# Strided v in four transfers of 32 partitions, and the weights' own parts stored in two transfers

## The chip, the cores and the metric

The kernel runs on one core of one Trainium2 chip. The core has a matrix engine (PE in the profile; its weight loads are PEld), three engines for elementwise work (DVE, ACT, POOL) and SyncE (SP), which here does nothing but issue transfers. Transfers between device memory and the core's working memory run on 16 DMA engines. The working memory has 128 partitions; a tile is named by its partitions times its bytes in each.

The metric is the device time of one execution in microseconds (us), as the median of several runs. Less is better.

## What is computed

Attention over 8 batches, 8 heads, 576 positions and a head size of 64, with two kinds of mask, and behind it a feed-forward layer with three input matrices whose products are joined by a maximum. In the reference (cut):

```python
mask_local = (rel >= 0) & (rel < stride)                     # heads 0 to 3, stride 32
mask_strided = (rel >= 0) & (pos[None, :] % stride == pos[:, None] % stride)   # heads 4 to 7
scores = np.where(masks[None, :, :, :], scores, -1000000000.0)
scores = scores - np.max(scores, axis=-1, keepdims=True)
attn = np.exp(scores)
attn = attn / (np.sum(attn, axis=-1, keepdims=True) + 1e-09)
attn_out = np.matmul(attn, v).astype(np.float32)

x = attn_out.transpose(0, 2, 1, 3).reshape(B * S, H * D)     # 4608 x 512
h = np.maximum(np.maximum(x @ w1, x @ w2), x @ w3)           # 512 x 768 each
return (h @ w_out).astype(np.float32)                        # 768 x 512
```

## The kernel before

**Units.** The attention is done in 32 units, each a batch `b` and a pair of heads `p`. Pairs 2 and 3 have the strided mask, pairs 0 and 1 the local one; in each batch the order is 2, 3, 0, 1, so units 4, 5, 8, 9, 12, 13 and so on are strided. For a unit, `load_qk` (L238) and `load_v` (L256) issue the transfers, `scores` (L303) makes the products of q and k on PE, DVE and ACT turn them into probabilities, and `values` (L428) multiplies by v. `paired_queries` (L292) rearranges q on ACT for strided units. `leading` and `rest` (L498 to L505) copy the result, on ACT and DVE, into the feed-forward's input. Each unit has a tile for q and k and one for v; of each there are two (plus two for units 2 and 3), so the loads of unit n + 2 are issued when unit n has been used.

**Numbers in parts.** Every float32 number that PE works on is the sum of two shorter ones, a high and a low part, and a product of two such numbers is three matmuls. The weights arrive as 64-bit words from which ACT, DVE and POOL build the two parts (`convert_begin` at L157 to `convert_end` at L199). There are 24 weight tiles, w0 to w17 for the three input matrices and six more for the output matrix. ACT reads a tile first at L164 as soon as it has landed, and works in order.

**Three stretches.** First, LOADS (L54) is a list of transfers, written out by hand, that SP issues at the start: q and k, v, and weights, step by step. Each token such as `v4` asks `load_v` for its next transfer; `q`, `w` and `v` mean qk, weights and v. OPENING (L58) is a list of computing steps in a fixed order, in which the weights are converted, the first units are done and the first 512 tokens pass through the feed-forward (`ff_in` at L518, `ff_max`, `ff_out`, `ff_store`). Second, a loop (L729) takes the next 512 tokens through it, with one unit of the attention between the products now and then (`burst`, L650). Third, `supers` (L772) takes the other 3,584 tokens in four groups with a scheme that needs seven products instead of eight for a 2 x 2 block of matrices. Before it, and between its groups, `conversion` (L679) prepares the group's input on ACT (L686) and DVE (L689, L692).

**Weights for the third stretch.** The scheme needs sums and differences of the weights. `build_sums` (L571), `build_mix`, `build_high` and `build_low` make them in nine builds in the first two stretches and store them in device memory, in `scratch`, a tensor of 9 builds x 128 partitions x 7 products x 512 numbers. Of the seven products four (S4, S2, S1, S3) are stored by `build_high` and `build_low` at L611 and L613. Three are the weights' own parts: A12 and A11, the two halves of one weight tile, are stored at L575, and A22, a half of another, at L576. `load_next` (L666) streams one product, 256 KB, back into a tile `w_stream` at L674; eight are kept ahead, and each of the third stretch's products (six matmuls at L778) uses one and calls `load_next` again. Outputs leave by transfers that ACT issues, at L563 and L876.

**Order.** `pin` keeps the program's order on each engine. SP is thus one queue: an issue that has to wait holds all that stand behind it. ACT's issues stand between its copies in the same way.

**The two places of the change.** A strided unit's v is, in device memory, a tensor of 32 rows (and unused ones up to 128) x 2 heads x 32 groups x 64 numbers. In working memory partition 32j + r holds, of row r, the groups 8j to 8j + 7 of both heads: 2 x 2 KB. For batch 0, where only 18 rows are read, `load_v` issues four transfers of 18 partitions (L285); from batch 1 on it issues one of 128 partitions (L279), whose source has j outermost. The own parts at L575 go out as they lie: 4 KB a partition, the high part of both halves and then the low part of both; `load_next` then picks the halves of A12 and A11 out of that order (L671), in two pieces of 1 KB a partition, while other products are read as one piece of 2 KB (L673).

Of the kernel before, what the change touches and what calls it, by code (L numbers as in the profile page):

```python
# [7 lines left out]
F32 = mybir.dt.float32  # L8
# [17 lines left out]
NI = S // STRIDE  # L26
# [7 lines left out]
PAIRED = 1  # L34
# [15 lines left out]
A12, A11, A22, S4, S2, S1, S3 = range(7)  # L50
# [21 lines left out]
def fused_kernel(ctx, tc, qT, kT, qk_loc, qk_str, v_loc, v_str, m_loc, m_str, w1, w2, w3, w_out, out):  # L72
    nc = tc.nc
# [9 lines left out]
    scratch = dram.tile([9, P, 7, 512], F32, name="scratch")  # L83
# [16 lines left out]
    pin = tc.keep_in_program_order  # L100
# [17 lines left out]
    for sign in (1, -1):  # L118
        pin(nc.gpsimd.affine_select(
            out=unit, in_=unit, pattern=[[-sign, P]], base=0, channel_multiplier=sign, compare_op=ALU.is_ge, fill=0.0  # L120
# [23 lines left out]
    def load_weights(count):  # L144
        for _ in range(count):
            i, j = sources.pop(0)
            raw = (wo if i is None else wt).tile([P, 1024], I32, name=f"w{i}_{j}")
            if i is None:
                pin(nc.sync.dma_start(out=raw, in_=w_out.bitcast(I32)[j * P : (j + 1) * P, :]))
            else:  # L150
                src = (w1, w2, w3)[i].bitcast(I32)[:, j * 2 * P : (j + 1) * 2 * P]
                pin(nc.sync.dma_start(
                    out=raw.rearrange("p (c f) -> p c f", c=NKC), in_=src.rearrange("(c p) f -> p c f", p=P)
                ))
            raws.append((raw, i, j))
# [19 lines left out]
    converted, kept = [], {}  # L175
# [80 lines left out]
    def load_v(n):  # L256
        if n >= len(units):
            return
        b, p = units[n]
        if n in (2, 3):  # L260
            vt = io_early.tile([P, 2 * (MB + 1) * D], F32, name="v_t", bufs=2)
        else:
            vt = io.tile([P, 2 * MS * D], F32, name="v_t", bufs=2)
        if p < 2:

            v_of[n] = v = vt[:, : 2 * (MB + 1) * D].rearrange("p (h m d) -> p h m d", h=2, m=MB + 1)
            last = 3 * MB
            for j in range(3):
                pin(nc.sync.dma_start(out=v[32 * j : 32 * (j + 1)], in_=v_loc[b, p, :32, :, j * MB : (j + 1) * MB + 1, :]))
                yield  # L270
            pin(nc.sync.dma_start(out=v[96:, :, : NT - last, :], in_=v_loc[b, p, :32, :, last:, :]))
            yield
            pin(nc.sync.dma_start(out=v[96:, :, NT - last, :], in_=v_loc[b, p, 32:, :, NT - 1, :]))
            yield
        else:
            v_of[n] = v = vt.rearrange("p (h m d) -> p h m d", h=2, m=MS)
            if b >= PAIRED:
                src = v_str[b, p - 2, :32].rearrange("r h (j m) d -> j r h (m d)", j=4)
                pin(nc.sync.dma_start(out=vt.rearrange("p (h x) -> p h x", h=2), in_=src))  # L279
                yield  # L280
                return
            for j in range(4):

                rows = NI
                pin(nc.sync.dma_start(  # L285
                    out=v[32 * j : 32 * j + rows], in_=v_str[b, p - 2, :rows, :, j * MS : (j + 1) * MS, :]
                ))
                yield
# [280 lines left out]
    halves = lambda x: x.rearrange("p (h f) -> p h f", h=2)  # L569

    def build_sums(q):  # L571

        _, j, i = builds[q]
        to = scratch[q].rearrange("p n (l f) -> p n l f", l=2)
        pin(nc.sync.dma_start(out=scratch[q][:, A12 : A11 + 1].rearrange("p n x -> p (n x)"), in_=kept[i, j].bitcast(F32).rearrange("p l x -> p (l x)")))  # L575
        pin(nc.sync.dma_start(out=to[:, A22], in_=kept[i, j + 1].bitcast(F32)[:, :, :256]))  # L576
        if q % 3 == 0:
            both = swp.tile([P, 2, 512], F32, name="sums_low")
            a = [both[:, n] for n in range(2)]
        else:  # L580
            a = [wk.tile([P, 512], F32, name="work") for _ in range(2)]
        a_of[q] = a
        for x, jj, engine in zip(a, (j, j + 1), (nc.gpsimd, nc.gpsimd)):
            parts = kept[i, jj].bitcast(F32)
            pin(engine.tensor_tensor(out=x, in0=parts[:, 0], in1=parts[:, 1], op=ALU.add))
# [30 lines left out]
    begun_loads = {}  # L616
    for step in LOADS.split():
        if step[0] == "w":
            load_weights(1)
        else:  # L620
            if step not in begun_loads:
                begun_loads[step] = {"q": load_qk, "v": load_v}[step[0]](int(step[1:]))
            next(begun_loads[step], None)
    load_weights(len(sources))
    steps = {
        "U": paired_queries, "S": scores, "X": less_maximum, "E": exponentials, "G": exponentials_apart, "N": lambda n: (probabilities(n), transposed(n)),
# [3 lines left out]
        "F": lambda n: ff_in(0, n // 3, n % 3), "f": lambda n: ff_in(0, n // 3, n % 3, (2, 3)),  # L630
        "g": lambda n: ff_in(0, n // 3, n % 3, (0, 1)), "M": lambda n: ff_max(0, n // 3, n % 3),
        "T": chunk_one, "Y": lambda n: (build_sums(n), build_mix(n)), "Z": lambda n: (build_high(n), build_low(n)),
        "O": lambda n: ff_out(0, n), "Q": lambda n: ff_store(0, n),
    }
    for step in OPENING.split():
        what, n = step[0], int(step[1:])
        steps[what](n)
        if what == "S" and n >= 4:
            list(load_qk(n + 2))
        if what == "V" and n >= 4:  # L640
            list(load_v(n + 2))
# [8 lines left out]
    def burst(n, alone=False):  # L650

        values(n)
        coming = n + 1 if n + 1 < len(units) and not alone else None
        if coming:
            scores(coming)
        list(load_v(n + 2))
        leading(n)
        rest(n)
        if coming:
            list(load_qk(coming + 2))  # L660
            less_maximum(coming)
        return coming
# [3 lines left out]
    def load_next():  # L666
        if to_load:
            _, q, m = to_load.pop(0)
            w = second["wst"].tile([P, 2, 256], F32R, name="w_stream")
            if m in (A12, A11):  # L670
                src = scratch[q][:, A12 : A11 + 1].rearrange("p l (n f) -> p n l f", n=2)[:, m]  # L671
            else:
                src = scratch[q][:, m].rearrange("p (l f) -> p l f", l=2)  # L673
            pin(nc.sync.dma_start(out=w.bitcast(F32), in_=src))  # L674
            stream.append(w)

    half = lambda blk, k: blk[:, 2:4, :] if k == 1 else blk[:, 0:2, :]
# [51 lines left out]
    for i in range(3 * NJ + CH // P):  # L729
# [19 lines left out]
        if i >= 3 * NJ:  # L749
            for _ in range((2, 0, 1, 1)[i - 3 * NJ]):  # L750
                next(convert, None)
            load_next()
            load_next()
# [3 lines left out]
        if i in sums_at:  # L757
            build_sums(sums_at[i])
            build_mix(sums_at[i])
# [12 lines left out]
    def supers():  # L772
# [32 lines left out]
        def quad(s, q):  # L805
# [6 lines left out]
            def go(out_, m, start=True):  # L812
                before(s, k[0])
                product(out_, m, x, stream.pop(0), start)
                load_next()
                after(s, k[0])
                k[0] += 1
# [149 lines left out]
```

## Time and profile before

The median of three runs is 730.75 us. The profile is of one more execution, the one that every row below comes from.

| | us |
|---|---|
| median of 3 runs (lowest, highest) | 730.75 (728.56, 733.78) |
| the profiled execution | 740.55 |
| its span, first to last instruction | 738.8 |
| strided v: transfers, KB each (batches 1 to 7) | 14, 512 |
| local v: transfers of 96, 48 and 16 KB | 48, 16, 16 |
| own parts: transfers of 512 KB, of 256 KB | 9, 9 |
| streamed weights: transfers of 256 KB | 252 |

The profiled execution took 1.3% longer than the median run, so shares are read from it, and differences of a few us with care.

Rows are read as follows. In the page, the second line gives the busy time of each engine; the chain that ended last is the work followed back from the last instruction through whatever released each step, and its shares say where the time went. DMA issues give the count, the size and the median time from issue to landing, where the trace has it. In the waits, a row names the engine and line that waited, who released it, the us in total, the times and the longest. In the timeline, a row has a start, a duration, the engine and the line, and in brackets the idle time before it and its releaser. In a table by stretches, each engine's busy time is followed by the clock that was granted to PE, the mean busy share of the 16 DMA engines, and GB/s.

### The profile page before, as it was taken

What the parts mean: (1) busy time and instruction counts of PE and PEld (TensorE: products, weight loads), DVE (VectorE), ACT (ScalarE), POOL (GpSimd) and SP (SyncE); (2) the same over time, 40 slices, a digit from 0 to 9 for tenths busy, and PEclk for the clock granted to TensorE, in tenths of its full rate; (3) what the DMA queues carried; (4) which work ended last, traced back from release to release, by engine and by line L of the source; (5) the groups of instructions that cost most, each with busy time, mean ns of one, the idle gap of its engine ahead of it and who ended that gap; (6) DMA issues with size and microseconds to landing.
All of it is one profiled execution on the core that took longest, in us unless ns stands there. A gap on an engine that the chain in (4) does not pass through costs nothing.

```text
span 738.8 us, 17982 instructions
## 1 busy us (share of the span) xinstructions
PE 667.8 (90%) x7408; PEld 571.8 (77%) x7408; DVE 375.7 (51%) x515; ACT 336.4 (46%) x702; POOL 300.7 (41%) x291
## 2 busy tenths in 40 slices
PE   4659998888997799889998899899999999999997
PEld 3548876666875688779787788788989988999986
DVE  6756963555561755446734445576264257034241
ACT  4747555332442544335544434455444446444441
POOL 8649895499760123223012323210332430344310
PEclk9989999897999699999999999999999999999999
DMA  9789414776787567777337777871686752677501
GB/s 288 184 228 296 131 60 150 248 235 211 263 286 213 168 219 233 180 185 248 120 114 192 168 230 247 203 161 71 169 274 188 206 151 86 176 219 217 171 32 69
DMA packets 94145, 138.35 MB, mean 187 GB/s; under 512 B 9168, under 2 KB 52432, under 8 KB 94064
## 3 DMA queue, kind: packets, MB, share of 16 engines
q1 hardware_dynamic: 88880, 127.76, 59.2%
q10 hardware_dynamic: 5184, 9.44, 3.4%
q8 instruction: 59, 0.97, 0.6%
q14 instruction: 22, 0.18, 0.1%
HBM read 111.21 MB, written 25.95 MB: 186 GB/s over the span
## 4 chain that ended last, share of the span: by engine, by line
PE 68%; DMA 18%; issue 4%; DVE 3%; SPq 3%; ACT 2%; POOL 1%; ACTq 1%; DVEq 0%; POOLq 0%
PE f_ps L778 35%; PE f_ps L868 14%; PE f_ps L527 12%; DMA w_stream<-scratch 7%; DMA w<-in_w 4%; DMA v_t<-in_v_str 4%; PE o_ps L475 2%; PE s_ps L345 2%; PE s_ps L323 2%; DMA qk_t<-in_qT 1%; PE o_ps L446 1%; SPq L246 1%; DVE h_all L835 1%; ACTq L563 1%; POOL snap L833 1%
## 5 line engine op out<-in xcount | busy, mean ns | idle before, releaser
L778 PE MATMUL f_ps<-xc,w_stream 128*128 128x448 f32 x1512 | 326.0, 376 | 25.3 <-DMA w_stream<-scratch 14.1
L778 PEld LDWEIGHTS f_ps<-xc,w_stream 128*128 128x128 f32 x1512 | 289.9, 193 | 55.0 <-issue 17.4
L821 ACT COPY snap<-f_ps 128x448 f32<-128x448 f32 x240 | 128.0, 534 | 182.2 <-PE f_ps L778 181.2
L833 POOL TENSOR_TENSOR snap<-snap 128x448 f32<-128x448 f32 x72 | 90.1, 1258 | 170.1 <-ACT snap L821 110.8
L835 DVE TENSOR_TENSOR h_all<-h_all,snap 128x448 f32<-128x448 f32 x96 | 82.9, 906 | 119.1 <-POOL snap L833 118.9
L833 POOL TENSOR_TENSOR h_all<-snap 128x448 f32<-128x448 f32 x36 | 41.3, 1148 | 186.2 <-ACT snap L821 185.0
L868 PE MATMUL f_ps<-wNone,h_parts 128*128 128x512 f32 x504 | 115.7, 390 | 1.1 <-ACT h_parts L858 1.1
L868 PEld LDWEIGHTS f_ps<-wNone,h_parts 128*128 128x128 f32 x504 | 94.3, 188 | 21.7 <-ACT h_parts L858 1.9
L527 PE MATMUL f_ps<-xh,w 128*128 128x512 f32 x288 | 100.3, 422 | 7.5 <-ACT xh L500 7.5
L527 PEld LDWEIGHTS f_ps<-xh,w 128*128 128x128 f32 x288 | 58.6, 204 | 21.6 <-ACT xh L500 7.9
L527 PE MATMUL f_ps<-xl,w 128*128 128x512 f32 x144 | 59.9, 416 | 0.1
L689 DVE TENSOR_TENSOR xc<-x_block,xc 128x896 fp32r<-128x896 f32 x28 | 29.8, 1087 | 25.8 <-ACT xc L686 25.8
L366 DVE TENSOR_TENSOR s_ps<-s_ps,mpair 128x576 f32<-128x576 f32 x14 | 10.7, 764 | 59.9 <-PE s_ps L323 59.9
L859 DVE TENSOR_TENSOR h_parts<-h_all,h_parts 128x768 fp32r<-128x768 f32 (+2 forms) x40 | 27.2, 712 | 26.0 <-ACT h_parts L858 25.7
L366 DVE TENSOR_TENSOR s_ps<-s_ps,mloc 128x640 f32<-128x640 f32 x14 | 11.6, 831 | 48.0 <-PE s_ps L345 46.2
L874 ACT COPY work<-f_ps 128x512 f32<-128x512 f32 x28 | 16.4, 587 | 41.8 <-PE f_ps L868 41.8
L527 PEld LDWEIGHTS f_ps<-xl,w 128*128 128x128 f32 x144 | 29.5, 205 | 6.6 <-DVE xl L505 0.6
L345 PE MATMUL s_ps<-qk_t 64*32 64x64 f32 (+1 forms) x1408 | 20.2, 232 | 14.5 <-DMA qk_t<-in_kT 7.6
L409 DVE STREAM_TRANSPOSE pt<-s_ps 128x640 f32<-128x640 f32 (+2 forms) x32 | 32.5, 1016 | 1.1
L858 ACT CAST h_parts<-h_all 128x768 fp32r<-128x768 f32 (+2 forms) x40 | 24.5, 642 | 17.7 <-DVE h_all L835 11.1
L389 ACT ACTIVATE s_ps<-s_ps 128x640 f32<-128x640 f32 (+2 forms) x30 | 19.5, 651 | 27.5 <-DVE s_ps L373 27.5
L557 PE MATMUL f_ps<-wNone,hh 128*128 128x512 f32 x96 | 31.6, 411 | 0.0
(87 smaller groups left out, 714.0 us busy)
## 6 DMA issues: line engine op xcount, KB each, us to landing
w_stream<-scratch SPq DMA_DIRECT2D x252, 256.0 KB, 3.7
w<-in_w SPq DMA_DIRECT2D x18, 512.0 KB, 13.5
out<-work ACTq DMA_DIRECT2D x36, 256.0 KB, 2.0
qk_t<-in_qT SPq DMA_DIRECT2D x28, 288.0 KB, 6.7
qk_t<-in_kT SPq DMA_DIRECT2D x28, 288.0 KB, 3.4
v_t<-in_v_str SPq DMA_DIRECT2D x14, 512.0 KB
v_t<-in_v_loc SPq DMA_DIRECT2D x48, 96.0 KB, 3.6
scratch<-w SPq DMA_DIRECT2D x9, 512.0 KB, 10.6
```

The source lines that it names most:

```text
L345: pin(nc.tensor.matmul(s_ps[32 * j : 32 * (j + 1), h, k1 : k1 + w], t[hs, q0 : q0 + 32], t[hs, k0 : k0 + w], start=not first, stop=not fir ...
L409: pin(nc.vector.transpose(pt[:, :, : nm * at], s_ps[:, :, : nm * at]))
L527: pin(nc.tensor.matmul(f_ps, w[:, kc, :], x[:, kc, :], start=(kc == 2 and n == 0), stop=(kc == 1 and n == 2)))
L557: pin(nc.tensor.matmul(f_ps, h[:, ts], w, start=(j == 0 and n == 0), stop=(j == NJ - 1 and n == 2)))
L689: pin(nc.vector.tensor_tensor(out=x[m][:, 1], in0=src, in1=x[m][:, 0].bitcast(F32), op=ALU.subtract))
L778: pin(nc.tensor.matmul(out_, w[:, wl, fs], x[:, xl, k, :], start=start and k == 0 and n == 0, stop=k == 1 and n == 2, skip_group_check=not ...
L821: pin(nc.scalar.copy(out=t, in_=src))
L833: pin(nc.gpsimd.tensor_tensor(out=h if i == 0 else u, in0=u, in1=t, op=ALU.add))
L835: pin(nc.vector.tensor_tensor(out=h, in0=h, in1=u, op=ALU.max))
L858: pin(nc.scalar.copy(out=to[:, 0, j0:j1], in_=src))
L859: pin(nc.vector.tensor_tensor(out=to[:, 1, j0:j1], in0=src, in1=to[:, 0, j0:j1].bitcast(F32), op=ALU.subtract))
L868: pin(nc.tensor.matmul(outs[t], h, w, start=(j == 0 and n == 0), stop=(j == NJ - 1 and n == 2)))
```

## The change

Strided v of batches 1 to 7 is loaded as that of batch 0: in four transfers, one for each j, of 32 partitions with 4 KB each, 128 KB a transfer. The tokens `v4` and `v5` in LOADS stand there four times already; until now the first issued the whole load and the three others nothing. The weights' own parts are stored so that high and low part of one product lie side by side: two transfers, one for the high and one for the low parts, each of two 1 KB pieces a partition, instead of one with 4 KB a partition. All products are then read back alike, in one piece of 2 KB a partition.

```diff
             v_of[n] = v = vt.rearrange("p (h m d) -> p h m d", h=2, m=MS)
-            if b >= PAIRED:
-                src = v_str[b, p - 2, :32].rearrange("r h (j m) d -> j r h (m d)", j=4)
-                pin(nc.sync.dma_start(out=vt.rearrange("p (h x) -> p h x", h=2), in_=src))
-                yield
-                return
             for j in range(4):
 
-                rows = NI
+                rows = NI if b < PAIRED else 32
                 pin(nc.sync.dma_start(
                     out=v[32 * j : 32 * j + rows], in_=v_str[b, p - 2, :rows, :, j * MS : (j + 1) * MS, :]
                 ))
@@ build_sums
-        pin(nc.sync.dma_start(out=scratch[q][:, A12 : A11 + 1].rearrange("p n x -> p (n x)"), in_=kept[i, j].bitcast(F32).rearrange("p l x -> p (l x)")))
+        for n in range(2):
+            pin(nc.sync.dma_start(out=to[:, A12 : A11 + 1, n], in_=halves(kept[i, j].bitcast(F32)[:, n])))
         pin(nc.sync.dma_start(out=to[:, A22], in_=kept[i, j + 1].bitcast(F32)[:, :, :256]))
@@ LOADS
-            next(begun_loads[step], None)
+            next(begun_loads[step])
@@ load_next
-            if m in (A12, A11):
-                src = scratch[q][:, A12 : A11 + 1].rearrange("p l (n f) -> p n l f", n=2)[:, m]
-            else:
-                src = scratch[q][:, m].rearrange("p (l f) -> p l f", l=2)
-            pin(nc.sync.dma_start(out=w.bitcast(F32), in_=src))
+            pin(nc.sync.dma_start(out=w.bitcast(F32), in_=scratch[q][:, m].rearrange("p (l f) -> p l f", l=2)))
```

## The prediction

> **What bounds the kernel now.** I read the page's engine line, the chain that ended last and the DMA issues first, then the waits of TensorE (PE) and of SyncE's queue (SP), then the timeline at each place those waits named.
>
> ```profile
> PE 667.8 (90%) x7408; PEld 571.8 (77%) x7408; DVE 375.7 (51%) x515; ACT 336.4 (46%) x702; POOL 300.7 (41%) x291
> ...
> PE 68%; DMA 18%; issue 4%; DVE 3%; SPq 3%; ACT 2%; POOL 1%; ACTq 1%; DVEq 0%; POOLq 0%
> ...
> v_t<-in_v_str SPq DMA_DIRECT2D x14, 512.0 KB
> v_t<-in_v_loc SPq DMA_DIRECT2D x48, 96.0 KB, 3.6
> ```
>
> PE is busy 667.8 of 738.8 us, so 71 us is all that removing waits can give, beside work done at a lowered clock. The second line says DMA carries 18% of the chain, so those waits are largely transfers. The last two lines are the two kinds of v load.
>
> ```profile
> PE f_ps L778 <- DMA w_stream<-scratch: 14.1, 4, 4.6
> PE f_ps L527 <- ACT xh L500: 7.5, 1, 7.5
> ...
> PE f_ps L778 <- ACT work L562: 6.5, 1, 6.5
> ...
> PE s_ps L323 <- ACT pt L300: 3.8, 2, 2.8
> PE o_ps L446 <- ACT x_block L603: 2.9, 1, 2.9
> ...
> PE f_ps L778 <- DVE xc L689: 2.2, 1, 2.2
> ```
> ```profile
> SPq L674 <- DMA v_t<-in_v_str: 34.3, 7, 6.7
> ```
>
> These six waits of PE are 37 us (us in all, times, longest), and all of them begin while a strided v load is under way or just after. SP's own list says it outright: it stands 34.3 us at L674, the issue of the next streamed weight, until an earlier v_str has landed. Why it must wait is seen by counting in the timeline: DMAs take eight completion counters in turn, so the issue that comes eight later waits for the landing of the one before it on that counter.
>
> ```profile
> core 0: us, PE busy (x) PEld busy (x) DVE busy (x) ACT busy (x) POOL busy (x), PEclk, DMA share, GB/s
> 113.00:117.00 4.00, 4.00 (x19) 3.23 (x18) 0.00 (x0) 2.76 (x13) 3.43 (x5) 1.00 0.25 77
> 292.00:301.00 9.00, 8.61 (x42) 7.43 (x40) 5.34 (x8) 5.77 (x13) 3.49 (x3) 1.00 1.06 189
> 274.94:287.30 12.36, 12.36 (x68) 11.19 (x72) 8.00 (x11) 5.40 (x10) 5.12 (x5) 1.00 0.82 268
> ```
>
> The first row is the tail of a v_str issued at 108.97: the DMA share is 0.25, so four engines of 16 work and twelve are idle, at 77 GB/s. In the second another v_str shares the engines with streamed weights: they are all busy, yet move 189 GB/s. The third follows a local v load: less busy, 268 GB/s. The one-transfer v is narrow, and it drags what it is mixed with.
>
> **The change, part by part.**
>
> *Strided v, 1 transfer to 4.* 14 transfers become 56; the same 2 KB pieces, 32 partitions a transfer. In the opening only the first of four v4 (and v5) steps issues now, so nothing is moved there, but three issues are added ahead of w9 and ahead of w14. After that, three are added ahead of the qk loads, the builds' stores or the streamed weights.
>
> ```profile
> L279 SPq DMA_DIRECT2D v_t<-in_v_str x14: 590/593/622, 35.9 to 479.3; - x14
> ```
>
> Each added issue costs SP about 0.6 us: 3 x 0.59 = 1.8 us a load, 14 x 1.8 = 25 us in all. The price of a landing is bounded by rows: a 96 KB, 32-partition local piece lands in 3.6 us, a one-transfer v_str in 9.4 to 12.6 (chain rows below). A piece here is 128 KB; I take 4, so that v is complete 1.8 + 4 = about 6 us after its first issue. It is nearest to the local piece, as its shape on the chip side is the same.
>
> *The streams (stage of L778).*
>
> ```profile
> 273.49 1.85 SPq L269 DMA_DIRECT2D v_t<-in_v_loc  x3
> ...
> 278.24 8.25 SPq L674 DMA_DIRECT2D w_stream<-scratch  x10
> 288.41 0.61 SPq L279 DMA_DIRECT2D v_t<-in_v_str  x1
> ...
> 290.39 16.03 SPq L674 DMA_DIRECT2D w_stream<-scratch  x10
> ```
> ```profile
> 274.94 12.36 PE f_ps L778 x60
> ...
> 290.39 13.24 DMA w_stream<-scratch
> 303.76 4.24 PE f_ps L778 x12
> ...
> 323.65 4.04 PE f_ps L778 x12
> ...
> 405.31 3.86 PE f_ps L778 x12
> ...
> 426.25 4.21 PE f_ps L778 x12
> ```
>
> Behind the local load (three rows of it at L269, two more issues at L271 and L273) ten weights go out in 8.25 us; behind v_str ten take 16.03, and the first needs 13.24 to land. A product is six matmuls, 12.36/10 = 1.24 us, and eight are kept ahead: 9.9 us of cover. 13.2 - 9.9 = 3.3, which is a stall of 14.1/4 = 3.5 us. With v complete after 6 us the cover holds, as it does behind the local loads, which have five issues, one more than the new strided ones. What is late next there is nothing until a load takes 9.9 us. Each stall also leaves PE at a lowered clock: 12 matmuls should take 12 x 0.206 = 2.47 and take 4.24, 4.04, 3.86 and 4.21, together 6.5 us too much. Term: 14.1 + 6.5 = 20.6.
>
> *The opening.*
>
> ```profile
> 36.54 12.37 SPq L152 DMA_DIRECT2D w<-in_w  x5
> ```
> ```profile
> 50.10 0.66 ACT L164 ACTIVATE work<-w 128x512 f32<-128x512 f32 x1 [8.25 <-DMA w<-in_w]
> ```
> ```profile
> 52.41:58.32 5.91, 5.80 (x13) 4.22 (x14) 4.63 (x8) 4.64 (x9) 5.13 (x7) 0.50 0.83 259
> 64.00:70.00 6.00, 6.00 (x87) 4.86 (x86) 4.86 (x7) 3.54 (x9) 5.81 (x6) 1.00 0.97 346
> ```
>
> v4 is issued at 35.88 and w9 right behind it; five issues that should cost 0.5 each take 12.37, and w9 lands at 50.1. ACT works in order, so its copy xh waits behind w9, and PE behind xh (the 7.5). With v4 spread, w9 is issued 1.8 later and, with 1.6 MB (qk, v, w9) moving at the 346 GB/s of the last row in 4.7 us from 36.5 on, lands at 42 to 44: 6 to 7.5 us of the stall go. The clock after it (0.50 for 5.9 us) gives up to 2.95 more. But POOL converts the weights and is busy 5.81 of 6 us in the last row, so it, not PE, is late next and I don't count all of 10.4. Term: 8.
>
> *Two ACT stalls.*
>
> ```profile
> 115.96 4.50 ACTq L563 DMA_DIRECT2D out<-work  x1
> ...
> 138.49 1.33 ACT L300 COPY pt<-qk_t 128x288 f32<-128x288 f32 x4 [5.12 <-DMA v_t<-in_v_str]
> ```
> ```profile
> 128.62 9.41 DMA v_t<-in_v_str
> ```
> ```profile
> 124.64:130.00 5.36, 5.36 (x155) 4.61 (x156) 3.27 (x4) 2.69 (x8) 5.28 (x5) 0.68 0.85 285
> 139.59:143.65 4.06, 4.06 (x69) 3.51 (x70) 2.02 (x3) 1.31 (x4) 0.00 (x0) 0.58 0.48 156
> ```
>
> An output's issue on ACT takes 4.50 us while the narrow v_str drains; another waits for v_str's counter for 5.1 us. Behind them stand L603 and L300 and, behind these, PE (2.9 and 2.8 us). After either the clock falls to 0.68 and 0.58 (last rows): 5.36 x 0.32 and 4.06 x 0.42, 1.7 us lost each time. Landing 3 to 4 us sooner covers 2.9 and nearly 2.8. Terms: 4.5 and 4.
>
> *The border of the stages.*
>
> ```profile
> 225.98 12.63 DMA v_t<-in_v_str
> ```
> ```profile
> 231.71 0.59 ACT L562 COPY work<-f_ps 128x512 f32<-128x512 f32 x1 [7.02 <-DMA w_stream<-scratch]
> ...
> 239.07 1.78 ACT L686 CAST xc<-x_block 128x896 fp32r<-128x896 f32 x2 [6.77 <-DMA v_t<-in_v_str]
> ```
>
> ACT stands 7.0 + 6.8 us behind two v_str counters; the conversions at L686 then hold PE (6.5 us, then 2.2 for DVE). SP's 2 x 1.8 extra come on the path here, since from 208 to 220 it issues without a pause; the four pieces of 225.98 would start about 223 to 225 and land by 230. L686 then starts near 230.5. Term: 8.5.
>
> *Own parts in two transfers.* Nine stores of 512 KB become 18 of 256 KB, and their reads go from two pieces of 1 KB a partition to one of 2 KB.
>
> ```profile
> L575 SPq DMA_DIRECT2D scratch<-w x9: 332/450/1159, 109.7 to 207.0; - x9
> ```
>
> Nine issues more, 9 x 0.45 = 4 us of SP. The cover: SP pauses for PE, ACT or POOL after every build but that at 207.0, where 0.45 is on the path (in the 8.5). The stores' shorter pieces and the reads' longer ones have no row of their own: from -2 us (72 lighter reads, in a stage that would no longer wait for them) to +4 (no cover); I take 0, nearest to the neighbour L576, which already stores 1 KB pieces and has no one waiting for it.
>
> **Sum.** 20.6 + 8 + 4.5 + 4 + 8.5 = 45.6; I take off 5, as five terms will not all be whole: 41. The profiled execution took 740.55 (span 738.8), 9.8 above the median of 730.75, so it may hold longer waits than an ordinary run. I scale the gain by a tenth: 730.75 - 38 = 693.
>
> [...]
>
> **The rivals.**
>
> *Only the streams gain.* In the opening POOL, and at the border the extra issues and the chain of L686 and L692, may take the place of the waits. Then 20.6 and a few us: 706 to 716. For it: POOL's 5.81 of 6. Against: ACT's waits name v_str itself.
>
> *No change.* The pieces themselves, 2 KB at an 8 KB step in device memory, might be slow whatever engine takes them; then landings stay at 9 to 13 us, and so does 731. Against: 77 GB/s at a share of 0.25 is 19 for each busy engine, against 268/(16 x 0.82) = 20 in the third row.
>
> *Slower.* SP becomes the bound: four pieces take half of the eight counters and 1.8 us each time; if the cover of 9.9 us were under 1.8 + the landing, each load would lengthen the streams, and all 25 us of issues plus 4 of the stores would show: 760. It decides when pieces land later than 8 us. Against it: five-issue local loads pass without a stall.
>
> [...]
>
> **How the numbers follow.** The forecast, 693, has 0.68, with 679 (all terms whole, cold clock too: 52) to 706. Only the streams: 0.18. No change: 0.09. Slower: 0.05. The range 679 to 714 takes in most of the first two, 0.8. One per cent (7.3 us) is about what a measurement of this kernel can tell from no change; faster by more than that 0.87, within 0.09, slower 0.04.
>
> **What would show it.** v_str as 56 issues of 128 KB landing in about 4 us; no wait of SP at L674 for v_str; PE's wait for w_stream under 2 us; ten weights behind a strided load out in about 8 us; no 4.5 us issue at L563; w9 landed by 44; DMA under 12% of the chain. It would be wrong if the pieces land in over 8 us, if POOL keeps PE waiting from 45 to 110 us, or if L686 still starts after 236.

## The result, and the profile after

The changed kernel takes 701.15 us (median of 4 runs, 698.28 to 702.77) against 732.26 for the kernel before beside it on the same chip (728.56 to 738.40): a ratio of 0.956, with a 95% interval of 0.949 to 0.964. In a later group of runs on one chip it takes 698.92 against 735.24, a ratio of 0.952 (0.947 to 0.956). The gain is thus 31 to 36 us, where the prediction said 38; the forecast of 693 lies 8 us too low, the time inside the range of 679 to 714. The kernel before is not equally fast in every group of runs: its medians in the four groups of this document are 732.26, 735.24, 735.96 and 738.16.

The profiled execution of the changed kernel took 699.94 us, its span 698.2. From its page, the busy line, the chain that ended last and three DMA issues (count, KB each, median us from issue to landing):

```profile
PE 653.6 (94%) x7408; PEld 561.4 (80%) x7408; DVE 378.2 (54%) x515; ACT 336.8 (48%) x702; POOL 299.8 (43%) x291
...
PE 80%; DMA 8%; issue 5%; DVE 3%; SPq 2%; ACT 1%; POOL 1%; DVEq 0%; POOLq 0%; ACTq 0%
...
w_stream<-scratch SPq DMA_DIRECT2D x252, 256.0 KB, 3.2
w<-in_w SPq DMA_DIRECT2D x18, 512.0 KB, 5.0
...
v_t<-in_v_str SPq DMA_DIRECT2D x56, 128.0 KB, 3.6
```

PE does the same 7408 matmuls in 653.6 us where it took 667.8. As they are the same instructions, the 14.2 us are put down to the clock that was granted to PE (0.94 before and 0.99 after in the stretch from 100 to 234 us of before, 0.96 and 0.99 in the streams). The rest of the span, in which PE stands, falls from 738.8 - 667.8 = 71.0 to 698.2 - 653.6 = 44.6 us, by 26.4. Together these are the 40.6 us between the two spans: two thirds are waits, one third is the clock (in the traces' records of it, 0.50 stands in 11 stretches of before and in 4 of after, the last us of both left out). DMA holds 8% of the chain instead of 18%. A quarter of a strided v lands 3.6 us after its issue. That is a median: by the last updates of their counters in the trace, the four quarters of the second load in the opening took 8.5 to 10.2.

The waits of PE in the changed kernel, its largest ones in the places that the prediction named (us in all, times, longest):

```profile
PE s_ps L318 <- issue: 3.1, 2, 2.9
...
PE f_ps L770 <- DVE xc L681: 2.5, 1, 2.5
PE f_ps L770 <- issue: 2.4, 2, 2.1
PE f_ps L522 <- ACT h_max L537: 2.1, 1, 2.1
...
PE f_ps L522 <- ACT xh L495: 1.0, 1, 1.0
PE s_ps L318 <- ACT pt L295: 1.0, 1, 1.0
...
PE f_ps L770 <- ACT work L557: 0.7, 1, 0.7
```

The wait of 14.1 us for streamed weights is not in the list any more. The 7.5 behind xh are 1.0, the 3.8 behind pt are 1.0, the 6.5 behind ACT's copy are 0.7, and x_block's 2.9 are gone. The 2.2 behind DVE's xc, which the prediction counted among the waits for v, are still there (2.5). New is a wait of 2.1 behind h_max, in the opening. SP's own waits, the two largest at the issue of streamed weights:

```profile
SPq L666 <- PE f_ps L770: 224.1, 182, 26.7
...
SPq L666 <- DMA w_stream<-scratch: 16.1, 6, 6.3
```

SP waited 34.3 us here for an earlier v_str; that row is gone, and what is left at L666 is almost all waiting for PE, as it should be where PE sets the pace. The timeline of SP's queue in the opening and in the third stretch shows why (start, duration, issues):

```profile
35.72 2.49 SPq L280 DMA_DIRECT2D v_t<-in_v_str  x4
38.25 3.78 SPq L152 DMA_DIRECT2D w<-in_w  x5
...
287.16 2.81 SPq L280 DMA_DIRECT2D v_t<-in_v_str  x4
...
291.11 8.77 SPq L666 DMA_DIRECT2D w_stream<-scratch  x10
```

The five weights behind v go out in 3.78 us, not 12.37, and ten streamed weights behind a strided v in 8.77, not 16.03. The table by stretches has the stretch of that last row (PE, PEld, DVE, ACT and POOL busy, granted clock, DMA share, GB/s):

```profile
core 0: us, PE busy (x) PEld busy (x) DVE busy (x) ACT busy (x) POOL busy (x), PEclk, DMA share, GB/s
291.00:300.00 9.00, 9.00 (x46) 8.11 (x45) 7.27 (x9) 5.73 (x13) 3.94 (x4) 1.00 0.93 319
```

The same mixture of strided v and streamed weights that moved 189 GB/s at a share of 1.06 now moves 319 at 0.93, and PE has no gap. What is left of the old waits stands on ACT, in its timeline:

```profile
115.91 0.34 ACTq L558 DMA_DIRECT2D out<-work  x1
...
126.46 1.34 ACT L295 COPY pt<-qk_t 128x288 f32<-128x288 f32 x4 [0.81 <-DMA qk_t<-in_qT]
...
219.00 0.58 ACT L557 COPY work<-f_ps 128x512 f32<-128x512 f32 x1 [7.87 <-DMA v_t<-in_v_str]
...
220.00 1.78 ACT L678 CAST xc<-x_block 128x896 fp32r<-128x896 f32 x2 [0.41 <-ACT work L557]
```

ACT's issue of an output takes 0.34 us where it took 4.50, and the wait of 5.12 before L295 is 0.81, for q instead of v. At the border of the stages ACT had two waits of 7.0 and 6.8 us. One of them is left, 7.87 for a piece of v; the second is gone, and the conversions start at 220.00.

### The profile page after: what moved, and what is told of

It is laid out like the page before. It is cut to its first block, busy times and chain, and to the rows that moved or that the text cites. A ratio compares the mean times of both kernels' runs of the same rounds, so it can differ in the third digit from the quotient of the medians.

```text
span 698.2 us, 18038 instructions
## 1 busy us (share of the span) xinstructions
PE 653.6 (94%) x7408; PEld 561.4 (80%) x7408; DVE 378.2 (54%) x515; ACT 336.8 (48%) x702; POOL 299.8 (43%) x291
## 4 chain that ended last, share of the span: by engine, by line
PE 80%; DMA 8%; issue 5%; DVE 3%; SPq 2%; ACT 1%; POOL 1%; DVEq 0%; POOLq 0%; ACTq 0%
PE f_ps L770 42%; PE f_ps L860 15%; PE f_ps L522 13%; DMA w<-in_w 4%; PE f_ps L552 3%; PE o_ps L470 2%; PE o_ps L441 2%; PE s_ps L318 2%; PE s_ps L340 2%; DMA w_stream<-scratch 1%; DMA v_t<-in_v_str 1%; DMA scratch<-work 1%; DVE h_all L827 1%; POOL snap L825 1%; SPq L152 1%
## 5 line engine op out<-in xcount | busy, mean ns | idle before, releaser
L770 PE MATMUL f_ps<-xc,w_stream 128*128 128x448 f32 x1512 | 318.2, 371 | 7.1 <-DVE xc L681 2.5
L770 PEld LDWEIGHTS f_ps<-xc,w_stream 128*128 128x128 f32 x1512 | 285.0, 190 | 34.8 <-ACT snap L813 3.4
L522 PE MATMUL f_ps<-xh,w 128*128 128x512 f32 x288 | 97.6, 412 | 3.1 <-ACT h_max L537 2.1
L522 PEld LDWEIGHTS f_ps<-xh,w 128*128 128x128 f32 x288 | 56.6, 196 | 16.8 <-ACT h_max L537 2.5
L522 PE MATMUL f_ps<-xl,w 128*128 128x512 f32 x144 | 58.4, 406 | 0.4 <-DVE xl L500 0.4
```

Of the source, the lines that this page charges most:

```text
L522: pin(nc.tensor.matmul(f_ps, w[:, kc, :], x[:, kc, :], start=(kc == 2 and n == 0), stop=(kc == 1 and n == 2)))
L770: pin(nc.tensor.matmul(out_, w[:, wl, fs], x[:, xl, k, :], start=start and k == 0 and n == 0, stop=k == 1 and n == 2, skip_group_check=not ...
```

## The experiments

The theory: the gain is the strided load alone, because each of its transfers now gets all 16 DMA engines in place of four, and the waits behind it go in each stage as priced. The rivals: the own parts have a share in it or cost something; the number of transfers or of issues on SP is what counts; or the pieces in device memory are slow whatever carries them. Each experiment is a kernel with one thing altered. Times are medians with the lowest and highest run; a ratio is to the kernel before on the same chip in the same group of runs.

### The two halves of the change apart

Strided v in four transfers, own parts stored in one as before (run twice). The cut shows the stores; the reads in `load_next` are as before too:

```diff
-        for n in range(2):
-            pin(nc.sync.dma_start(out=to[:, A12 : A11 + 1, n], in_=halves(kept[i, j].bitcast(F32)[:, n])))
+        pin(nc.sync.dma_start(out=scratch[q][:, A12 : A11 + 1].rearrange("p n x -> p (n x)"), in_=kept[i, j].bitcast(F32).rearrange("p l x -> p (l x)")))
```

> Strided v in four transfers, own parts stored and read as before. Theory (the v load is the whole gain): 701 to 705 us, as the changed kernel. Rival (the reads of A12 and A11 in 1 KB pieces held the streams up): 710 to 722, as half of the gain or more would be missing.

Own parts in two transfers, strided v in one as before:

```diff
+            if b >= PAIRED:
+                src = v_str[b, p - 2, :32].rearrange("r h (j m) d -> j r h (m d)", j=4)
+                pin(nc.sync.dma_start(out=vt.rearrange("p (h x) -> p h x", h=2), in_=src))
+                yield
+                return
```

> Own parts in two transfers and read in 2 KB pieces, strided v in one transfer as before. Theory: no change beyond 1 per cent, 726 to 738 us, with PE's wait for w_stream near the 14 us of before. Rival (the parts bring half): 710 to 722.

Measured: v alone 698.76 us (696.43 to 702.59), ratio 0.947 (0.940 to 0.954), a little under the 701 to 705 expected. Own parts alone 736.77 (730.07 to 743.97, 10 runs), ratio 1.000 (0.995 to 1.006). Waits of the second of them, PE's first, then SP's:

```profile
PE f_ps L775 <- DMA w_stream<-scratch: 12.0, 5, 3.8
...
PE f_ps L527 <- ACT xh L500: 2.6, 1, 2.6
```
```profile
SPq L671 <- DMA v_t<-in_v_str: 32.7, 7, 6.4
```

The waits that the change removes all stand in the kernel that has only the own parts changed. The whole gain, as far as these runs can tell, is the load of v. The row of 2.6 behind xh shows something else: this wait, 7.5 in the profile of before, is not the same in every run.

Whether the own parts cost a little was asked once more, with more runs in one group:

> The changed kernel once more, as the measure for the other runs of this group on the same chip. All theories: 699 to 703 us and a ratio of 0.95 to 0.96 to the kernel before, with no row of PE behind w_stream over 1 us.

> Strided v in four transfers, own parts in one transfer per core as before. The first run of this arrangement gave 698.76 us, the changed kernel 701.15. Theory (the own parts' half of the change is worth nothing): within 1% of changed_again, that is less than 3 us apart, with intervals of the ratios that overlap. Rival (the own parts in two transfers cost something, since they add instructions on the issuing queue): this run is faster than changed_again by 2 to 4 us and the intervals of the ratios stand apart.

The changed kernel took 698.92 (695.96 to 701.22), v alone 698.68 (694.89 to 702.28), with ratios of 0.952 (0.947 to 0.956) and 0.952 (0.948 to 0.957). The own parts' half is worth nothing that six runs of each can show.

### Number of transfers, or number of engines?

The prediction read a DMA share of 0.25 as four engines of 16, and the source of that transfer is led by j, which is 4 long. That the first comes from the second was the author's guess. If so, the count of transfers is beside the point. Two transfers of 64 partitions, each led by a dimension of 2, should then be worse than one. (The lines taken out are those of the kernel before; the rest is the changed kernel, here and in the next one.)

```diff
-                src = v_str[b, p - 2, :32].rearrange("r h (j m) d -> j r h (m d)", j=4)
-                pin(nc.sync.dma_start(out=vt.rearrange("p (h x) -> p h x", h=2), in_=src))
-                yield
+                for i in range(2):
+                    src = v_str[b, p - 2, :32, :, 16 * i : 16 * (i + 1)].rearrange("r h (j m) d -> j r h (m d)", j=2)
+                    pin(nc.sync.dma_start(out=vt[64 * i : 64 * (i + 1)].rearrange("p (h x) -> p h x", h=2), in_=src))
+                    yield
```

> The changed kernel, but strided v of batches 1 to 7 in two transfers of 64 partitions, each with a source led by a dimension of 2. Theory (the leading dimension sets how many engines work): two engines carry 512 KB, so a load takes about twice the 9.4 to 12.6 us of the four-engine one, 18 us or more; each of six loads in the streams then waits 18 - 9.9 = 8 us or more instead of 3.5, and the kernel is slower than before: 770 us or more. Rival (what counts is that the load is cut into smaller transfers): between 701 and 731, about 715.

And one transfer should be as good as four, if its source is led by the partitions. For that the input holds a second copy of strided v, laid out partition by partition, with an unused group after each head so that the pieces stay 2 KB:

```diff
-                src = v_str[b, p - 2, :32].rearrange("r h (j m) d -> j r h (m d)", j=4)
+                src = v_pair[b, p - 2][:, :, :MS].rearrange("p h m d -> p h (m d)")
```

> The changed kernel, but strided v of batches 1 to 7 in one transfer of 128 partitions from an input laid out partition by partition, in the same 2 KB pieces. Theory (engine count, not the number of transfers): as the changed kernel or up to 1 per cent less, 694 to 702 us, since 42 issues of 0.6 us go as well; v_str lands in about 4 to 6 us. Rival (one large transfer ahead of the streamed weights is what blocks them): 725 to 735.

Measured: two transfers 804.91 us (801.86 and 807.95), ratio 1.090 (1.079 to 1.102). One wide transfer 692.99 (692.30 to 694.78), ratio 0.939 (0.933 to 0.945), 1 us under the range expected. The issue of one strided v in the kernel with two transfers, three of its stretches behind a strided v (the first of them behind this one), and then its largest wait of PE:

```profile
260.61 1.63 SPq L280 DMA_DIRECT2D v_t<-in_v_str  x2
```
```profile
core 0: us, PE busy (x) PEld busy (x) DVE busy (x) ACT busy (x) POOL busy (x), PEclk, DMA share, GB/s
263.00:267.00 4.00, 0.00 (x0) 0.00 (x0) 0.00 (x0) 0.00 (x0) 0.00 (x0) 0.50 0.13 50
367.00:371.00 4.00, 0.00 (x0) 0.00 (x0) 0.00 (x0) 0.00 (x0) 0.00 (x0) 0.58 0.13 46
442.00:446.00 4.00, 4.00 (x20) 3.72 (x21) 2.49 (x3) 1.86 (x4) 0.00 (x0) 1.00 0.12 35
```
```profile
PE f_ps L776 <- DMA w_stream<-scratch: 55.0, 6, 14.4
```

A share of 0.12 to 0.13 is two engines of 16, at 35 to 50 GB/s; in the first two stretches PE, DVE, ACT and POOL all stand still. By the last updates of their counters in the trace, both transfers were under way in the first and the third stretch (in the second the later one alone). With two transfers under way and a share of two engines, that fits both on the same two.

The traces have a second sign of the number of engines, which does not depend on what else is moving: how often the completion counter of a transfer is updated. It is 16 times for every quarter in the changed kernel (its source led by 32 rows) and for every wide transfer (by 128 partitions), but 5 times for every one-transfer v of the kernel before (by 4) and 3 times for each of the two here (by 2). That fits 16, four and two engines with one update each, and in the last two cases one update more.

The issues of the one wide transfer, from the page of its profile:

```profile
v_t<-in_v_pair SPq DMA_DIRECT2D x14, 512.0 KB, 4.4
```

Same bytes, pieces of 2 KB, same number of issues as before, and a landing after 4.4 us instead of 9.4 to 12.6. The two pieces of a partition are 2,304 bytes apart in device memory here and 8 KB before; but the changed kernel leaves them at 8 KB, and its quarters land in 3.6. So neither the pieces nor the transfer's size made it slow, but the engines it was given: two, 805 us; four, 738; sixteen, 693. In the same group four transfers took 698.76, so that one wide transfer is 5.8 us better than four.

The kernel before with nothing but the wide transfer (one piece of 4 KB a partition here, own parts as before):

```diff
-                src = v_str[b, p - 2, :32].rearrange("r h (j m) d -> j r h (m d)", j=4)
+                src = v_pair[b, p - 2].rearrange("p h m d -> p h (m d)")
```

> The kernel before, with strided v of batches 1 to 7 in one transfer of 128 partitions from an input laid out partition by partition, 4 KB a partition without a gap; own parts as before. Theory (both halves of the change are beside the engine count): 688 to 695 us, as with 2 KB pieces or a little less. Rival (the own parts' layout is worth something once v is fast): 698 to 704.

It took 695.11 (690.94 to 701.77), ratio 0.944 (0.935 to 0.953), at the upper end of the 688 to 695 expected. Either kernel with the wide transfer beats the kernel before; that it beats the changed one is shown for the first of the two, whose runs all lie below those of four transfers.

### Eight transfers: does SP become the bound?

The slower case of the prediction was that SP's issues would show. Eight transfers of 16 partitions put 56 more on its queue:

```diff
+            if b >= PAIRED:
+                for i in range(8):
+                    rs = slice(16 * (i % 2), 16 * (i % 2 + 1))
+                    pin(nc.sync.dma_start(out=v[16 * i : 16 * (i + 1)], in_=v_str[b, p - 2, rs, :, i // 2 * MS : (i // 2 + 1) * MS, :]))
+                    if i % 2:
+                        yield
+                return
```

> Strided v in eight transfers of 16 partitions each in place of four: 56 more issues, by 0.6 us each some 33 us more on SP's queue over the whole kernel. Theory (what counts is that each transfer is spread over all 16 DMA engines, and SP's issuing is hidden behind PE): within 1.5% of changed_again, that is 695 to 712 us, the row of PE behind w_stream below 3 us. Rival (the number of transfers or of issues costs, the slower case of the prediction): 10 us or more slower than changed_again, with waits of PE for v, for the conversions or for w_stream of 5 us and more.

Measured: 718.88 us (717.70 to 720.24), ratio 0.980 (0.975 to 0.984). That is 20 us above the changed kernel of the same group. The theory fails here and the rival has the right sign and size, but not by the waits that it named: none of PE's waits for v, the conversions or w_stream reaches 5 us. The page's busy line and chain, then a piece of the chain that ended last:

```profile
PE 665.3 (93%) x7408; PEld 570.4 (80%) x7408; DVE 376.5 (53%) x515; ACT 336.5 (47%) x702; POOL 299.6 (42%) x291
...
PE 75%; DMA 7%; SPq 6%; issue 5%; DVE 3%; ACT 2%; POOL 1%; ACTq 0%; DVEq 0%; POOLq 0%
```
```profile
208.24 0.56 SPq L280
...
213.14 0.59 SPq L280
...
216.18 1.45 SPq L616
...
217.69 1.00 SPq L673
```

SP has 6% of the chain (2% in the changed kernel), and before the border of the stages the chain runs through its queue from 204 to 223 us: eight issues for v from 208.24 to 213.73, and four more from 219.53 on, on the path of everything behind them. That is the place where the prediction put the extra issues on the path. The larger part of the 16.5 us between the spans (716.0, and 699.5 for the changed kernel in this group) is the clock, though: PE is busy 665.3 us here and 654.2 there with the same matmuls, 11.1 more; it stands 50.7 us here and 45.3 there, 5.4 more. Paired matmul by matmul, as in the listings further below, 7.3 us are lost between 100 and 234 us of before, where that piece of the chain lies, and 8.2 in the streams, for which no cause is shown. Why the granted clock is lower here (a mean of 0.956 over the profiled execution, 0.971 in the changed kernel of this group) was not tried.

### How much each stage held

The changed kernel with the narrow transfer put back for some batches only: batch 1 (the opening), batches 2 to 4 (two ACT stalls and the border), or batches 5 to 7 (the streams).

```diff
+            if b == 1:
+                src = v_str[b, p - 2, :32].rearrange("r h (j m) d -> j r h (m d)", j=4)
+                pin(nc.sync.dma_start(out=vt.rearrange("p (h x) -> p h x", h=2), in_=src))
+                yield
+                return
```

> The changed kernel, with the one-transfer v kept for batch 1 alone (units 4 and 5, issued in the opening). Theory (the prediction's terms add up): the opening's term comes back, 8 us by the prediction, 5 by the shift of PE between the two profiles: 705 to 710 us. Rival (POOL holds the opening whatever v does): under 703.

> The changed kernel, with the one-transfer v kept for batches 2 to 4 (units 8, 9, 12, 13, 16, 17, issued between the opening and the border of the stages). Theory: the two ACT stalls and the border come back, 17 us by the prediction, 14 by the shift of PE between the profiles: 713 to 720 us. Rival (other waits stand in the same places): under 708.

> The changed kernel, with the one-transfer v kept for batches 5 to 7 (units 20, 21, 24, 25, 28, 29, issued in the streams). Theory: 20.6 us by the prediction's term, so 718 to 724 us, with four waits of PE for w_stream of 14 us in all. Rival (the stalls in the streams were largely a result of earlier delays): under 710.

| narrow again for | median us (range) | above 701.15 | PE busy, standing (us) | terms of the prediction |
|---|---|---|---|---|
| none (the changed kernel) | 701.15 (698.28 to 702.77) | | 653.6, 44.6 | |
| batch 1 | 705.90 (703.11 to 707.00) | 4.8 | 656.0, 49.3 | 8 |
| batches 2 to 4 | 710.93 (708.63 to 714.79) | 9.8 | 652.3, 56.8 | 4.5 + 4 + 8.5 = 17 |
| batches 5 to 7 | 713.59 (710.09 to 716.09) | 12.4 | 656.5, 57.8 | 20.6 |

Busy and standing time are of the profiled executions (the second is span less busy). The ranges of all three lie above that of the changed kernel, so each stage holds something. Two of the three expectations were missed: 710.93 lies under 713 to 720, and 713.59 under 718 to 724, each above what its rival named. With four runs each, in another group than the changed kernel's (before took 735.96 beside these and 732.26 beside that), the sizes carry a few us of scatter. The waits that came back, in the kernels in this order, and for the first the timeline of SP:

```profile
36.28 0.61 SPq L279 DMA_DIRECT2D v_t<-in_v_str  x1
36.94 12.90 SPq L152 DMA_DIRECT2D w<-in_w  x5
```
```profile
PE f_ps L527 <- ACT xh L500: 8.3, 1, 8.3
```
```profile
PE f_ps L775 <- ACT work L562: 10.1, 2, 7.3
PE s_ps L323 <- ACT pt L300: 5.4, 2, 4.4
```
```profile
PE f_ps L775 <- DMA w_stream<-scratch: 13.2, 5, 3.4
```

Each is a wait that the prediction had named for its stage: 8.3 for 7.5 in the opening, 10.1 for 6.5 and 5.4 for 3.8 in the middle, 13.2 for 14.1 in the streams. One did not come back: x_block's 2.9 is 0.4 in the second kernel. What comes back with them is PE's standing time: 4.7, 12.2 and 13.2 us. What does not come back is the clock: PE's busy time moves by 2.4, -1.3 and 2.9 us, where before and after differ by 14.2. Ordinary medians (4.8 + 9.8 + 12.4 = 27.0) hold less than the profiles, as shown below.

### The wait left in the opening

Of the changed kernel's PE waits 3.1 us in the opening (1.0 behind xh, 2.1 behind h_max) are for ACT, which there waits for w9, w11 and w12. The loads of w9 to w13 put ahead of v:

```diff
-q4 q4 v4 v4 v4 v4 w9 w10 w11 w12 w13 q5 q5 v5 v5 v5 v5
+q4 q4 w9 w10 w11 w12 w13 v4 v4 v4 v4 q5 q5 v5 v5 v5 v5
```

> The changed kernel with the loads of w9 to w13 issued ahead of the four transfers of v for the fifth group of the opening, in place of behind them. In the changed kernel PE still stands 1.0 us behind xh and 2.1 us behind h_max in the opening, the second because ACT waited for w12 to land. Theory (those waits are the order of the queue, not the transfers' price): both rows go below 0.5 us or move behind v, and the time is 2 to 3 us below changed_again. Rival (another engine sets the opening's end, or PE then waits for v by as much): within 1 us of changed_again, with a new row of PE or ACT behind v.

It took 697.84 (694.98 to 704.43), ratio 0.952 (0.947 to 0.956), against 698.92 at the same ratio. Nothing can be told apart. A wait of PE behind h_max is still there:

```profile
PE f_ps L522 <- ACT h_max L537: 0.9, 1, 0.9
```

In the profile of the changed kernel taken in this group neither wait, for xh or for h_max, was there at all, and it took no less time. So these 3 us come and go between executions, and these runs can't show that the order of the queue is worth anything.

## Why the prediction was right, and where it was off

The mechanism was right in the main, and the runs with the narrow transfer put back show it stage by stage. The eight counters that it names are in the trace of before: its 523 transfers from SP and ACT name eight, 65 or 66 times each, and of the 515 that find their counter used already 505 come eight transfers after its last use. In the streams, the streamed weight that has v's counter begins 0.06 us after that counter's last update, all six times. The landing, taken as 4 us, was 3.6. The row of SP behind v_str went, w_stream's wait fell to none, ten weights behind a strided load went out in 8.77 us ("about 8"), ACT read w9 at 43.24 ("landed by 44"), the 4.50 us issue on ACT became 0.34, DMA fell to 8% of the chain ("under 12%"), and L686, now L678, starts at 220.00, which with the 12.7 us gained ahead of it (below) is 232.7 in the time of before, against 239.07 then and 230.5 as predicted. Several terms of the sum were made up of other parts than the prediction said, and the largest was read from an execution that was unusual in just that stage.

PE's 7408 matmuls can be paired in order in the two traces, and the start of one in before less that of the same one in after tells how much has been gained up to there. What PE's busy time fell by in a part is put down to the clock; the rest is standing time. (Ordinary listings, this one and the next, worked out from the traces, to some tenths.)

```
start before  start after  gained  in this part: busy + standing                      predicted
    100.00        94.92       5.1       5.1  =  0.2 +  4.9   opening                  8
    234.02       221.32      12.7       7.6  =  6.0 +  1.6   first and second stretch 4.5 + 4
    248.26       229.19      19.1       6.4  =  0.5 +  5.9   border                   8.5
    500.01       459.44      40.6      21.5  =  7.5 + 14.0   streams                  20.6
```

The profiles of the experiments can be paired with that of before in the same way, part by part:

```
gained on the profile of before    opening   to 234 us   border   streams
changed kernel, as above               5.1         7.6      6.4      21.5
changed kernel, second profile         6.5         4.9      6.4      22.2
one wide transfer                      6.4        10.3      9.8      21.5
own parts alone                        0.8        -3.2      1.0       7.5
narrow again for batch 1              -0.3         2.8      7.0      23.8
narrow again for batches 2 to 4        6.4         2.5     -0.8      21.7
narrow again for batches 5 to 7        7.0         6.5      6.4       4.7
```

Where the narrow transfer is put back, that stage's gain goes, and most of the others' stays (batch 1 also costs some of the gain behind the opening).

**The streams: right in this pair of profiles, too large for others.** The gain is 21.5 for 20.6. But own parts alone has the same narrow loads as before and is 7.5 us shorter there, so that against it the changed kernel gains 14.0. The narrow transfer put back for batches 5 to 7 costs 21.5 - 4.7 = 16.8 in the profiles, and 12.4 in the medians. The term of 20.6 is thus 4 to 8 us too large for these.

**The opening: too large by 3 in this profile.** The wait behind xh went from 7.5 to 1.0, as much as was said, but nearly nothing came from the clock (0.2). The prediction said that POOL would be late next. In this profile it was the next weights on the same queue: ACT waited 1.58 us for w11 and 1.09 for w12, and PE 2.1 behind h_max. The second profile of the changed kernel has neither wait and gains 6.5, so part of the 3 us may be scatter.

**The two ACT stalls: the number near, its make-up not.** 7.6 us for 8.5, and x_block's wait of 2.9 and pt's of 2.8 went as said. But PE's waits that no engine explains ("issue") grew from 5.5 to 9.1 us in this part, so that its standing time fell by 1.6 only; the other 6.0 are busy time, where the prediction had counted 1.7 twice for the clock. That the sum came out is luck: the second profile gains 4.9 here.

**The border: too large by 2.** The term of 8.5 held two waits of PE, 6.5 behind ACT's copy and 2.2 behind DVE's xc. The first fell to 0.7, the second stayed at 2.5: it did not hang on the narrow load. The prediction also took both of ACT's long waits for v's counters; the row of the first (7.02) names a streamed weight. One of 7.87 for a piece of v is left in the changed kernel, now hidden for PE but for 0.7 us. With one wide transfer the border gains 9.8, which is 3.4 us more; that the extra issues of four transfers, which the prediction put on the path here, make this difference would fit and was not tried by itself.

**The own parts: nothing, as taken.**

**The sum, and how it was scaled.** The terms came to 45.6, with 5 taken off 41, and the profiled executions differ by 740.55 - 699.94 = 40.6. For "I scale the gain by a tenth" the prediction took off 3 (a tenth of 41 would be 4), which gave 38. The measured gain is 31.1 in the first group and 36.3 in the later one. So the sum fits the one execution that it was read from and is too large for the medians, after the 3 us still by 7 us or by 2. The listing points to the term: own parts alone, in a profile of 734.24 us, is 7.5 us shorter in the streams than before, 4.3 of it in PE's busy time. The streams' price, waits and clock, is thus what the runs show as mis-sized, more than the way of scaling it.

The price of the clock stays open. Over the whole kernel PE is busy 665.0 us with own parts alone, 11.4 more than in the changed kernel (before: 14.2), and the prediction counted it at each stall (6.5 in the streams, 1.7 at each of ACT's two). Yet the narrow transfer put back stage by stage brought back 30.1 us of standing time in all and only 4.0 of busy time. A stall is not followed by the same loss each time, and no run here shows what decides it.

**The rivals.** No change, because the pieces are slow: excluded by the changed kernel itself, which reads the same pieces from the same places and has them in 3.6 us. Only the streams: excluded by the two runs with the narrow transfer in the other stages. Slower through SP: not with four transfers. With eight the mechanism is there, though they still leave the kernel 2% faster than before. The prediction put the point from which it decides at pieces landing later than 8 us; in the run with eight, whose pieces land after 2.8 us in the median, SP's issues themselves stood on the path before the border.

## What to carry to other kernels

Look at the DMA share while a transfer is alone: here it was 0.25 and 0.13, which times 16 is four and two engines, where the outermost dimension of the source was 4 and 2. That dimension is the first suspect. Before cutting a transfer into pieces, see whether its source can be laid out with the partitions outermost; here that is 5.8 us better than four pieces, and eight pieces are 20 us worse than four. (Either layout is made on the host, outside the time measured.) A profile is one execution: the streams of this one were 7.5 us longer than those of a kernel with the same loads. Read the price of a stall from more than one execution before adding it up.

## What the runs showed of the hardware that was not expected

**A narrow transfer holds up the issues behind it.** Behind one v_str of four engines, five issues of weights took 12.37 us in before and 12.90 in the kernel with the narrow transfer back in the opening; behind four of 16 engines, 3.78. Whether it also holds up issues of another engine is not shown. One issue on ACT that began while a v_str drained took 4.50 us in before, and 0.34 in the changed kernel; but two others of before that began during a v_str of four engines took no longer than usual:

```profile
219.25 0.34 ACTq L563 DMA_DIRECT2D out<-work  x1
...
231.25 0.34 ACTq L563 DMA_DIRECT2D out<-work  x1
```

And in the kernel with one wide transfer the issue at the same place as the one of 4.50 took 1.71 us, after v had landed.

**Gaps of PE that no engine explains.** PE's rows named "issue" add up to 10.2 us in before and 14.1 in after (all rows of that name in the lists of waits), so that they are now PE's largest kind of gap. One of them cuts a run of 64 equal matmuls at the same place in two executions of the changed kernel, here the first:

```profile
128.71 0.76 PE L318 MATMUL s_ps<-qk_t,pt 64*64 64x36 f32 x37
132.36 0.56 PE L318 MATMUL s_ps<-qk_t,pt 64*64 64x36 f32 x25 [2.89 <-issue]
```

In the DMA queues of just that gap (129.47 to 132.36; packets, MB, share of 16 engines) stands one packet of the queue that the trace names instruction:

```profile
q8 instruction: 1, 0.02, 2.1%
```

In the second execution the gap is 4.26 us, after the same 37 matmuls, again with one such packet in it. What PE waits for there is not shown.
